# The three MLP blocks in two halves, with fewer and longer bursts of score maxima

## The chip, the cores and the metric

The kernel runs on one core of a Trainium2 chip. The time is the device time of that core in microseconds (us). The kernel before takes 1648.96 us, the median of three runs (1647.39 to 1649.14). The core's engines run their own instruction streams: TensorE (PE, with its weight loads shown as PEld), VectorE (DVE), ScalarE (ACT), GpSimd (POOL), and SyncE (SP), which here issues the DMAs. An engine takes its instructions in the order of the program, and waits where one needs the result of another engine.

## The reference: one transformer layer

For 2048 rows of 512 numbers:

```python
h   = x + attention(layernorm(x), wqkv) @ wo      # 32 heads of 16, softmax over all 2048 keys
out = h + silu(layernorm(h) @ w1) @ w2            # w1 is 512 x 1792, w2 is 1792 x 512
```

All arrays are float32, and the result has to keep float32 accuracy. The kernel therefore splits most operands of a product into a high and a low float16 part and adds three products (high with high, low with high, high with low).

## The kernel before, in words

**Attention.** The queries are taken in four blocks of 512 rows (`NB = 4`). Work is ordered in items: an item is four heads of one block, so there are 32 items (`ITEMS`), eight to a block. An item has 16 groups, one for each 128 keys (`KC = 16`). A group computes four score tiles of 128 keys by 512 queries (`scores`, line 414: one matmul and one exponential on ACT each), and, two groups later (`LAG = 2`), the products of the exponentials with the values (`values`, line 749), which add up in the PSUM bank `pv`.

**Maxima.** The exponential needs the maximum of each row of scores beforehand. `maximum` (line 259) computes a tile of 128 queries by 512 keys of the scores on PE, with 48 rows of contraction, into a PSUM bank, and DVE reduces it to one column (line 271). There are 64 such maxima to an item, 2048 in all. They run ahead of the attention that needs them, for items whose queries and keys are already loaded. When those of an item are complete, POOL turns them into two float16 rows (`finish_max`), and some steps later `place_max` transposes these on PE (`ps_n`), copies them on DVE (`mt`) and sends them by DMA into the query tile. Inside attention, a planner (`maxima`, line 1154) decides for each group how many maxima go beside its four scores, at most three, from the number still missing before each item's start; it takes off what the MLPs will do (`BESIDE`). `one_max` alternates between two heads whose rows lie in different halves of the array, rows 0 to 63 and 64 to 127. A maximum writes into one of the three `sm` banks in turn, or into a bank given by the caller.

**MLP.** When a block's attention is complete, its output projection and layer norm run beside the next block's first item, and the block's MLP runs in one piece at the start of the next item (`marks`: groups 144, 272 and 400; `finish_block`, line 1037, calls `mlp`, line 970). So three MLPs, called b = 0, 1, 2 here, stand between stretches of attention; the fourth, `finish_last`, ends the kernel and is written separately.

The MLP walks over the 1792 hidden features in 14 chunks of 128 (`FC = 14`). For chunk f, the *first product* is 12 matmuls of 128x128 by 128x512 (four slices of the 512 inputs, three float16 products each). `gate` then applies SiLU on ACT to a tile `g`, scales it to the high half of `gh` on ACT, and subtracts for the low half. The *second product* of the chunk (`second`, line 950) is again 12 matmuls, three for each 128 rows, into four banks `ps_acc`, in which all 14 chunks add up. Before the change, the loop runs first product of f, gate of f, second product of f - 1. The first product goes into `pv` (free at that time) and the four other banks of the kind `st` hold three accumulators and the chunk-0 product, then the fourth accumulator.

Between these matmuls stand bursts of maxima at fixed places (`BESIDE_C`): three after the 5th matmul of a first product, three after its 12th, and four after the 8th of a second product. `QUIET` leaves them out of the last three chunks of b = 2. At the end of each MLP eight scores of the coming groups are inserted.

**Order and time steps.** PE, ACT, DVE, POOL and SP instructions are kept in the order written. `tick()` counts steps, one for each chunk of the loop or group of attention, and `soon(n, ...)` puts off a small job by n steps: the placing of maxima, and the reciprocal of the softmax sums on POOL (`invert`, line 835) with its small DMAs.

**Weights.** The split w1 and w2 lie in DRAM and are loaded by `load_weights` into eight tiles of 256 KB (`raw_tile`), in the order of use. The exponentials and the gates' `gh` share a ring of tiles (`pt_tile`), twelve before the change (`PTS`).

Of the kernel before, what the change touches and what calls it, by code (L numbers as in the profile page):

```python
# [10 lines left out]
F32 = mybir.dt.float32  # L11
# [3 lines left out]
AF = mybir.ActivationFunctionType  # L15
ALU = mybir.AluOpType
# [4 lines left out]
P = 128  # L21
# [5 lines left out]
DC = D // P  # L27
FC = F // P
# [17 lines left out]


LAG = 2
PTS = 12

EARLY = 8

# [14 lines left out]
AHEAD = 4  # L67


BESIDE = (135, 135, 103)  # L70
OUTPUT = 9

BESIDE_V = [(0, 0), (0, 4, 4, 4)], [(4, 4), (4, 4, 4, 4)], [(6, 6), (6, 6, 6, 5)]
# [4 lines left out]

BESIDE_A1 = 10, 9, 8, 7

BESIDE_C = {5: 3, 12: 3}, {8: 4}

MORE = 2, 2, 0

QUIET = FC, FC, FC - 3


@with_exitstack
def attention_mlp_kernel(ctx: ExitStack, tc: tile.TileContext, x, wqkv, wo, w1, w2, out):
# [5 lines left out]
    def mm(*a, **k):  # L95
        tc.keep_in_program_order(nc.tensor.matmul(*a, **k))  # L96
# [5 lines left out]
    def pool(op, *a, **k):  # L102
        tc.keep_in_program_order(getattr(nc.gpsimd, op)(*a, **k))  # L103


    def pin(ins):
        tc.keep_in_program_order(ins)

    def act(fn, *a, **k):
        pin(getattr(nc.scalar, fn)(*a, **k))  # L110

    def dve(fn, *a, **k):
        pin(getattr(nc.vector, fn)(*a, **k))  # L113

    def dma(*a):
        pin(nc.sync.dma_start(*a))

    def low(dst, src, high, engine="dve"):

        if high.dtype == F32R:  # L120
            high = high.bitcast(F32)
        (pool if engine == "pool" else dve)("tensor_tensor", dst, src, high, ALU.subtract)
# [6 lines left out]
    def product(ps, lh, ll, rh, rl, n, start=True, stop=True):  # L129

        k = 0
        for c in range(n):
            for a, b in ((lh, rh), (ll, rh), (lh, rl)):
                mm(ps, a(c), b(c), start=start and k == 0, stop=stop and k == 3 * n - 1)
                k += 1
                yield
# [3 lines left out]
    small = ctx.enter_context(tc.tile_pool(name="small", bufs=3))  # L140
# [7 lines left out]
    def bank(name, kind="st", dtype=F32):  # L148
        pool_of = banks[kind]
        if isinstance(pool_of, list):  # L150
            pool_of.append(pool_of.pop(0))
            return pool_of[-1].tile([P, 512], dtype, tag=pool_of[-1].name, name=name)
        return pool_of.tile([P, 512], dtype, tag=kind, name=name)

    ident = const.tile([P, P], F32, name="ident")
# [16 lines left out]
    h_f, g_s, out_f, wo_f, o_minus, o_twice = (factors[:, n:n + 1] for n in range(8, 14))  # L172
# [128 lines left out]
    def finish_rest():  # L301
        while unfinished:
            finish_max(unfinished.pop(), True)
# [31 lines left out]
    def tick():  # L335
        at["step"] += 1
        for step in [step for step in late if step < at["step"]]:

            finish_rest()
            for i in late.pop(step):  # L340
                place_max(i)
        for fn, a in agenda.pop(at["step"], ()):
            fn(*a)
# [49 lines left out]
    def burst(n, *more):  # L393
        for ps in more:
            one_max(ps=ps)
        for _ in range(n - len(more)):
            one_max()

    def weave(steps, inserts):

        for k, _ in enumerate(steps):
            if k + 1 in inserts:
                inserts[k + 1]()
# [6 lines left out]
    def pt_tile(name, dtype=F32):  # L410
        pool_of = pools[next(taken) % PTS >= EARLY]
        return pool_of.tile([P, 512], dtype, tag="pt", name=name)
# [13 lines left out]
    with ExitStack() as pa:  # L426
# [289 lines left out]
        for g in range(1, NG // 2):  # L716
            for m, (b, key) in enumerate([(b, 1) for b in range(NB)] + [(b, 0) for b in range(NB)]):
# [3 lines left out]
                n = 8 * g + m - 12  # L721
# [16 lines left out]
    pv = bank("pv", "pv")  # L738
    cpool = ctx.enter_context(tc.tile_pool(name="cpool", bufs=1, side="right"))
    bp = ctx.enter_context(tc.tile_pool(name="bp", bufs=PTS - EARLY))  # L740
    pools.append(bp)
    gp = ctx.enter_context(tc.tile_pool(name="gp", bufs=2))
# [4 lines left out]
    hth = cpool.tile([P, DC, 512], F16, name="hth")  # L747
    htl = cpool.tile([P, DC, 512], F16, name="htl")
# [120 lines left out]
    ws, hx, os = {}, {}, {}  # L869


    first_weights = {9: ("w1", 0), 12: ("w1", 1), 14: ("w2", 0), 15: ("w1", 2)}

    def raw_tile():
        return gp.tile([P, 512], F32, tag="w", name="w", bufs=8)

    def parts_of(w):
        return w.bitcast(F16).rearrange("p (s n) -> p s n", s=2)

    def load_weights(kind, f):  # L880
        if f < FC:
            w = parts_of(raw_tile())
            dma(w, wd[kind][f])
            ws[kind, f] = w[:, 0], w[:, 1]
# [55 lines left out]
    def turn_rows(t):  # L940
        turn(hx.pop(t), hth[:, :, t * P:(t + 1) * P], htl[:, :, t * P:(t + 1) * P])

    def gate(ps):
        g, parts = pt_tile("g"), parts_of(pt_tile("gh"))
        act("activation", g, ps, AF.Silu, scale=h_f)
        act("mul", parts[:, 0], g, g_s)
        dve("scalar_tensor_tensor", parts[:, 1], g, g_s, parts[:, 0], op0=ALU.mult, op1=ALU.subtract)
        return parts[:, 0], parts[:, 1]

    def second(b, acc, f, gh, gl, inserts={}):  # L950
        w2h, w2l = ws.pop(("w2", f))
        while f == 0 and len(acc) < 4:
            acc.append(bank("ps_acc"))
        steps = (product(acc[t], lambda c: gh[:, t * P:(t + 1) * P], lambda c: gl[:, t * P:(t + 1) * P],
                         lambda c: w2h, lambda c: w2l, 1, start=f == 0, stop=f == FC - 1) for t in range(4))
        if f < FC - 1:
            weave(chain.from_iterable(steps), inserts)
            return
        for t, step in enumerate(steps):
            weave(step, {k - 3 * t: fn for k, fn in inserts.items()})  # L960
            n = 4 * b + t
            h = rows_of(b, t)

            parts = 1 + (n == KC - 1)
            for m in range(parts):
                cols = slice(m * D // parts, (m + 1) * D // parts)
                dve("scalar_tensor_tensor", h[:, cols], acc[t][:, cols], out_f, h[:, cols], op0=ALU.mult, op1=ALU.add)
                dma(out[n * P:(n + 1) * P, cols], h[:, cols])

    def mlp(b):  # L970

        first = bank("ps_w1")
        acc = [bank("ps_acc") for _ in range(3)]
        waiting = None
        ahead = [(g, m ^ (g % 2)) for g in marks[b:b + 1] + [marks[b] + 1] for m in range(4)]

        def some_scores(n):
            for _ in range(n):
                scores(*ahead.pop(0), "sm")

        for f in range(FC):
            tick()
            beside_1, beside_2 = BESIDE_C if f < QUIET[b] else ({}, {})
            beside_1 = {k: (lambda n=n: burst(n)) for k, n in beside_1.items()}
            if f == 0 and beside_1:

                beside_1[3] = lambda: burst(4, pv)
                del beside_1[5]
            beside_2 = {k: (lambda n=n: burst(n, *[pv] * (n == 4))) for k, n in beside_2.items()}
            if f == FC - 1:  # L990
                beside_2 = {8: lambda: some_scores(3)}
            if f:
                load_weights("w1", f + 2)
                load_weights("w2", f + 1)
            w1h, w1l = (w.rearrange("p (c n) -> p c n", n=P) for w in ws.pop(("w1", f)))

            ps = pv if f else first
            weave(product(ps, lambda c: w1h[:, c, :], lambda c: w1l[:, c, :],
                          lambda c: hth[:, c, :], lambda c: htl[:, c, :], DC), beside_1)

            parts = gate(ps)
            if f == FC - 1:

                act("activation", small.tile([P, 1], F32, name="sw"), ident[:, :1], AF.Exp)
            if waiting:
                second(b, acc, *waiting, beside_2)
            waiting = f, *parts

        def last_scores():

            scores(*ahead.pop(0))
            scores(*ahead.pop(0), "sm")
            if f < QUIET[b]:
                burst(2)

        second(b, acc, *waiting, {2: lambda: some_scores(3), 10: last_scores})

    found = {}

# [17 lines left out]
    def finish_block(b, pending):  # L1037

        act("activation", small.tile([P, 1], F32, name="sw"), ident[:, :1], AF.Silu)
        load_weights("w2", 1)  # L1040
        for g in pending:
            values(g)
        mlp(b)
# [110 lines left out]
    def maxima(g):  # L1154
# [4 lines left out]
        ready = min(ITEMS, i + RING - (0 if c == KC - 1 else 1)) * 64  # L1159
        rate = max([(n - sum(x for x, m in zip(BESIDE, marks) if g <= m <= start) - at["done"])  # L1160
                    / max(1, start - AHEAD - g) for n, start in goals] or [0])
# [14 lines left out]
    for g in range(groups):  # L1176
        tick()
        i, c = divmod(g, KC)
# [5 lines left out]
        if g < DC:  # L1184
            w = raw_tile()
            dma(w, wo[g * P:(g + 1) * P, :])
            soon(8, split_wo, g, w)
        f, c4 = divmod(g - SPLIT, 4)
        if c4 == 0 and 0 <= f < 2 * FC:
            kind, f = ("w1", "w2")[f % 2], f // 2  # L1190
            soon(4, split_weights, kind, f, load_raw(kind, f))
        if i in FIRSTS:
            b, n = i // 8 - 1, c - OUTPUT
# [23 lines left out]
        n = maxima(g)  # L1217
# [9 lines left out]
        for m in range(4):  # L1227
            k = m ^ (g % 2)
# [50 lines left out]
```

## Time and profile before

| | |
|---|---|
| median of three runs | 1648.96 us (1647.39 to 1649.14) |
| the profiled execution | 1649.26 us |
| its span, first to last instruction | 1647.5 us |
| PE busy | 1624.0 us, 99% |
| DVE busy | 1439.0 us, 87% |
| ACT busy | 1206.6 us, 73% |
| POOL busy | 363.5 us, 22% |
| MLPs b = 0, 1, 2, from first product to last | 497.6 to 601.6, 867.8 to 971.7, 1236.7 to 1335.7 us |

Times in the profile count from the span's start. A line of the timeline gives the start, the length, the engine, the line of the kernel, the operation, what it writes and reads, and how many like it follow one another; a bracket at its end is idle time of the engine before it, and what ended that. Matmuls are pipelined: a 512-column matmul shows a length of 0.38 us, but the next may begin earlier, so starts tell more than lengths. `PEclk` is the clock granted to PE, where 1.00 is full speed.

### The profile page before, as it was taken

To read this page: it belongs to the slowest core of one execution; us is meant where nothing else is said; L and a number is where in the kernel's file an instruction comes from. 1 tells how busy PE (TensorE), PEld (TensorE's weight loads), DVE (VectorE), ACT (ScalarE), POOL (GpSimd) and SP (SyncE) were. 2 spreads that over 40 slices of the span, in tenths; PEclk is the share of its full clock that TensorE was granted. 3 is DMA by queue.
4 is the path that set the end of the run, shared out by engine and by line. 5 is a ranking of instruction groups with operands and counts; after the bars stand their busy time and mean duration, and the time that the engine had idled before them with its cause. 6 is when DMAs were issued, how large, how long until landed. Compare 5 with 4: busy or idle time off the path is not lost.

```text
span 1647.5 us, 28474 instructions
## 1 busy us (share of the span) xinstructions
PE 1624.0 (99%) x10553; PEld 516.1 (31%) x10553; DVE 1439.0 (87%) x2385; ACT 1206.6 (73%) x2391; POOL 363.5 (22%) x594
## 2 busy tenths in 40 slices
PE   9899999999999999999999999999999999999999
PEld 7566522222223322222223322222233322222254
DVE  7799999999999989999999989999988969999431
ACT  5445599999972169999972169999972179999732
POOL 4323354544421001121121001121121001111100
PEclk9999999999999999999999999999999999999999
DMA  5657344333432211111232211112132211100222
GB/s 192 170 142 220 100 96 121 99 107 107 117 76 85 71 51 32 34 36 49 54 76 85 70 51 32 33 36 53 51 77 90 65 50 32 36 12 21 72 81 73
DMA packets 100951, 125.91 MB, mean 76 GB/s; under 512 B 24144, under 2 KB 61072, under 8 KB 100812
## 3 DMA queue, kind: packets, MB, share of 16 engines
q1 hardware_dynamic: 100812, 124.10, 27.1%
q8 instruction: 82, 1.34, 0.3%
q14 instruction: 57, 0.47, 0.1%
HBM read 93.45 MB, written 24.63 MB: 72 GB/s over the span
## 4 chain that ended last, share of the span: by engine, by line
PE 79%; DVE 14%; ACT 4%; DMA 2%; issue 1%; POOL 0%; SPq 0%; DVEq 0%; ACTq 0%
PE pv L96 32%; PE ps_s L96 21%; DVE mx L271 11%; PE ps_m L96 10%; PE ps_qk L96 5%; PE ps_acc L96 4%; PE ps_w L96 3%; ACT pt L110 3%; PE ps_wo L96 2%; PE ps_v L96 2%; DVE gh L113 1%; DMA ks<-in_B_w_dram 1%; PE ps_tr L99 1%; DVE ot L113 0%; DVE pvs L113 0%
## 5 line engine op out<-in xcount | busy, mean ns | idle before, releaser
L271 DVE TENSOR_REDUCE mx<-ps_m 128x1 f32<-128x512 f32 x2011 | 1260.5, 683 | 68.1 <-PE ps_m L96 36.4
L110 ACT ACTIVATE pt<-ps_s 128x512 f32<-128x512 f32 x2048 | 1010.4, 608 | 30.0 <-PE ps_m L96 17.8
L96 PE MATMUL pv<-pt,va 128*17 128x512 f32 x4096 | 537.6, 598 | 0.9
L96 PE MATMUL ps_s<-qs,ks 64*128 64x512 f16 x2048 | 532.6, 379 | 2.0 <-ACT pt L110 0.5
L96 PE MATMUL ps_m<-ks,qs 48*128 48x512 f16 x2011 | 513.6, 381 | 9.0 <-DVE mx L271 6.1
L96 PEld LDWEIGHTS <-ks 64*128 64x128 f16 x2048 | 150.3, 95 | 550.0 <-issue 437.1
L110 ACT ACTIVATE g<-pv,factors 128x512 f32<-128x512 f32 x39 | 26.8, 688 | 217.5 <-PE pv L96 217.5
L96 PE MATMUL ps_acc<-w,gh 128*128 128x512 f16 x672 | 161.2, 380 | 0.0
L103 POOL TENSOR_TENSOR ri<-rc,minus 128x16 f32<-128x16 f32 x31 | 90.9, 2932 | 282.0 <-DMA rc<-dn 282.0
L96 PEld LDWEIGHTS <-qs 48*128 48x128 f16 x2048 | 119.6, 94 | 76.1 <-issue 70.1
L96 PEld LDWEIGHTS pv<-pt,va 128*17 128x17 f32 x4096 | 69.0, 95 | 215.3 <-issue 202.7
L103 POOL TENSOR_TENSOR mx<-mx 128x32 f32<-128x32 f32 x34 | 8.6, 254 | 403.5 <-DVE mx L271 402.0
L113 DVE SCALAR_TENSOR_TENSOR gh<-g,factors,gh 128x512 f16<-128x512 f32 x56 | 41.7, 745 | 63.7 <-ACT gh L110 63.7
L96 PEld LDWEIGHTS <-w 128*128 128x128 f16 x708 | 65.2, 98 | 93.6 <-issue 29.1
L96 PE MATMUL pv<-hth,w 128*128 128x512 f16 x312 | 92.9, 379 | 0.0
L96 PEld LDWEIGHTS <-gh 128*128 128x128 f16 x672 | 59.2, 98 | 95.1 <-issue 32.4
L110 ACT ACTIVATE ks<-ps_qk,qk_s 128x512 f32<-128x512 f32 x30 | 20.7, 689 | 53.3 <-PE ps_qk L96 45.7
L96 PE MATMUL pv<-htl,w 128*128 128x512 f16 x156 | 59.5, 381 | 0.0
L103 POOL TENSOR_SCALAR nm<-nm 128x16 f32<-128x16 f32 (+1 forms) x50 | 13.1, 261 | 198.7 <-DVE nm L282 195.7
L96 PE MATMUL ps_qk<-xth,wqk_h 128*128 128x512 f32 x128 | 53.6, 419 | 0.6 <-ACT va L110 0.6
L96 PE MATMUL ps_qk<-xth,wqk_l 128*128 128x512 f32 x128 | 50.7, 396 | 0.0
L103 POOL TENSOR_TENSOR sl<-ks,sh 128x512 f16<-128x512 f32 x30 | 34.8, 1161 | 70.4 <-ACT sh L110 56.9
(134 smaller groups left out, 1002.8 us busy)
## 6 DMA issues: line engine op xcount, KB each, us to landing
ks<-kd SPq DMA_DIRECT2D x120, 192.0 KB
w<-w1d SPq DMA_DIRECT2D x56, 256.0 KB
w<-w2d SPq DMA_DIRECT2D x56, 256.0 KB
ks<-in_B_w_dram SPq DMA_DIRECT2D x28, 256.0 KB
w<-in_B_w_dram SPq DMA_DIRECT2D x28, 256.0 KB
qs<-qd SPq DMA_DIRECT2D x128, 48.0 KB
kd<-sh SPq DMA_DIRECT2D x16, 256.0 KB
qd<-sh SPq DMA_DIRECT2D x16, 256.0 KB
```

Of the source, the lines that this page charges most:

```text
L96: tc.keep_in_program_order(nc.tensor.matmul(*a, **k))
L99: tc.keep_in_program_order(nc.tensor.transpose(*a))
L103: tc.keep_in_program_order(getattr(nc.gpsimd, op)(*a, **k))
L110: pin(getattr(nc.scalar, fn)(*a, **k))
L113: pin(getattr(nc.vector, fn)(*a, **k))
L271: pin(nc.vector.tensor_reduce(mx[piece][:, j, a % n, qt, kb:kb + 1], ps, axis=AX.X, op=ALU.max))
```

## The change

The MLPs' loop is cut in two. First all 14 first products and gates run; the 14 tiles `gh` stay in the ring, which grows from 12 to 16. Then all 14 second products run. `g` gets two tiles of its own. In these three MLPs the low half of `gh` is made on POOL in two operations (scale `g` in place, subtract the high half) instead of one on DVE; the last MLP keeps DVE. Each first product writes a bank of the kind `st` in turn instead of `pv`.

The bursts change with it. In the first half there is one burst of six after the 6th matmul of a first product, not at chunks 6 and 13, and in b = 2 not at chunks 0, 3, 6, 9 and 12; it writes `pv`, two `st` banks and the three `sm` banks. In the second half, bursts of four (`pv` and three `sm`) are spread evenly over the first 144 matmuls: 16, 15 and 13 of them in b = 0, 1, 2. The planner's `BESIDE` becomes 138, 134, 106; the counts that really run in the MLPs were 135, 135 and 107 and become 138, 134 and 106.

Weights are loaded in the order all w1, then all w2, one a step and five ahead of use. There are now 28 steps (`tick`) in an MLP instead of 14. The activation-table switch to the exponential comes after the last gate, at the middle of the MLP instead of near its end.

```diff
-PTS = 12
+PTS = 16
-BESIDE = (135, 135, 103)
+BESIDE = (138, 134, 106)
-BESIDE_C = {5: 3, 12: 3}, {8: 4}
+BURSTS_1 = ({f: 6 for f in range(FC) if f not in (6, 13)},) * 2 + ({f: 6 for f in range(FC) if f % 3},)
+BURSTS_2 = 16, 15, 13
+SPAN_2 = 12 * (FC - 2)
-QUIET = FC, FC, FC - 3
...
-    first_weights = {9: ("w1", 0), 12: ("w1", 1), 14: ("w2", 0), 15: ("w1", 2)}
+    first_weights = {9: ("w1", 0), 12: ("w1", 1), 14: ("w1", 2), 15: ("w1", 3)}
+    order = [(kind, f) for kind in ("w1", "w2") for f in range(FC)]
...
-    def gate(ps):
-        g, parts = pt_tile("g"), parts_of(pt_tile("gh"))
+    def gate(ps, engine="dve"):
+        g, parts = gp.tile([P, 512], F32, name="g"), parts_of(pt_tile("gh"))
         act("activation", g, ps, AF.Silu, scale=h_f)
         act("mul", parts[:, 0], g, g_s)
-        dve("scalar_tensor_tensor", parts[:, 1], g, g_s, parts[:, 0], op0=ALU.mult, op1=ALU.subtract)
+        if engine == "pool":
+            pool("tensor_scalar", g, g, g_s, 1.0, op0=ALU.mult, op1=ALU.mult)
+            low(parts[:, 1], g, parts[:, 0], "pool")
+        else:
+            dve("scalar_tensor_tensor", parts[:, 1], g, g_s, parts[:, 0], op0=ALU.mult, op1=ALU.subtract)
...
     def mlp(b):
...
-            ps = pv if f else first
+            ps = bank("ps_w1")
+            n = BURSTS_1[b].get(f, 0)
             weave(product(ps, lambda c: w1h[:, c, :], lambda c: w1l[:, c, :],
-                          lambda c: hth[:, c, :], lambda c: htl[:, c, :], DC), beside_1)
-
-            parts = gate(ps)
-            if f == FC - 1:
-
-                act("activation", small.tile([P, 1], F32, name="sw"), ident[:, :1], AF.Exp)
-            if waiting:
-                second(b, acc, *waiting, beside_2)
-            waiting = f, *parts
...
+                          lambda c: hth[:, c, :], lambda c: htl[:, c, :], DC),
+                  {6: lambda: burst(n, pv, bank("ps_m"), bank("ps_m"))} if n else {})
+            gates.append(gate(ps, "pool"))
+
+        act("activation", small.tile([P, 1], F32, name="sw"), ident[:, :1], AF.Exp)
+        acc = []
+        inserts = {SPAN_2 * (n + 1) // BURSTS_2[b]: lambda: burst(4, pv) for n in range(BURSTS_2[b])}
+        inserts[12 * (FC - 2) + 8] = inserts[12 * (FC - 1) + 2] = lambda: some_scores(3)
+        inserts[12 * (FC - 1) + 10] = last_scores
+        for f in range(FC):
+            tick()
+            next_weights()
+            second(b, acc, f, *gates[f], {k: inserts[12 * f + k] for k in range(1, 13) if 12 * f + k in inserts})
...
-        load_weights("w2", 1)
+        load_weights("w1", 4)
```

More of the change, by code (lines that the diff above doesn't have):

```diff
@@ L970, in mlp, with next_weights @@
     def mlp(b):
-        first = bank("ps_w1")
-        acc = [bank("ps_acc") for _ in range(3)]
-        waiting = None
         ahead = [(g, m ^ (g % 2)) for g in marks[b:b + 1] + [marks[b] + 1] for m in range(4)]
+        weights = iter(order[5:])
+        def next_weights():
+            for kind, f in weights:
+                load_weights(kind, f)
+                return
         def some_scores(n):
@@ L979, in some_scores @@
                 scores(*ahead.pop(0), "sm")
[L981 to L989, printed above, removed]
-            if f == FC - 1:
[L991 to L995, printed above, removed]
-            ps = pv if f else first
-            weave(product(ps, lambda c: w1h[:, c, :], lambda c: w1l[:, c, :],
-                          lambda c: hth[:, c, :], lambda c: htl[:, c, :], DC), beside_1)
-            parts = gate(ps)
-            if f == FC - 1:
-                act("activation", small.tile([P, 1], F32, name="sw"), ident[:, :1], AF.Exp)
-            if waiting:
-                second(b, acc, *waiting, beside_2)
-            waiting = f, *parts
         def last_scores():
@@ L1012, in last_scores @@
             scores(*ahead.pop(0), "sm")
-            if f < QUIET[b]:
+            if b < 2:
                 burst(2)
-        second(b, acc, *waiting, {2: lambda: some_scores(3), 10: last_scores})
+        gates = []
+        for f in range(FC):
+            tick()
+            next_weights()
+            w1h, w1l = (w.rearrange("p (c n) -> p c n", n=P) for w in ws.pop(("w1", f)))
+            ps = bank("ps_w1")
+            n = BURSTS_1[b].get(f, 0)
+            weave(product(ps, lambda c: w1h[:, c, :], lambda c: w1l[:, c, :],
+                          lambda c: hth[:, c, :], lambda c: htl[:, c, :], DC),
[6 more added lines that the diff above has]
+        inserts[12 * (FC - 1) + 10] = last_scores
+        for f in range(FC):
+            tick()
+            next_weights()
+            second(b, acc, f, *gates[f], {k: inserts[12 * f + k] for k in range(1, 13) if 12 * f + k in inserts})
     found = {}
```

## The prediction

> **What bounds the kernel now.** I read the page's engine shares first, then a table of stretches for the places that the change touches and for an attention between them, then one period of an MLP in the timeline.
>
> ```profile
> PE 1624.0 (99%) x10553; PEld 516.1 (31%) x10553; DVE 1439.0 (87%) x2385; ACT 1206.6 (73%) x2391; POOL 363.5 (22%) x594
> ```
>
> PE looks full everywhere, so only a stage's own rows tell its limit. The stretches (columns: time, then busy time of each engine with its instructions, granted clock, DMA share, GB/s):
>
> ```profile
> core 0: us, PE busy (x) PEld busy (x) DVE busy (x) ACT busy (x) POOL busy (x), PEclk, DMA share, GB/s
> 497.60:601.60 104.00, 102.76 (x485) 34.05 (x480) 94.03 (x153) 25.42 (x39) 8.40 (x22) 1.00 0.22 65
> ...
> 975.00:1205.00 230.00, 229.55 (x1757) 51.50 (x1753) 220.23 (x359) 229.29 (x467) 38.90 (x62) 1.00 0.18 44
> ```
>
> In attention (975 to 1205) ACT works 229.29 of 230 us: 467 exponentials and copies of 0.491 us set the pace, and PE keeps up. Nothing in the change shortens ACT's work there, so attention gains nothing. In the MLP ACT works only 25 of 104 us, PE nearly all, DVE 94. The clock is 1.00 in both. What PE spends in the MLP is read from one period (chunk 5 or so of b = 0):
>
> ```profile
> 527.17 0.38 PE L96 MATMUL pv<-htl,w 128*128 128x512 f16 x1
> ...
> 527.48 0.60 PE L96 MATMUL ps_m<-ks,qs 48*128 48x512 f16 x3
> ...
> 527.91 1.89 DVE L271 TENSOR_REDUCE mx<-ps_m 128x1 f32<-128x512 f32 x3 [0.50 <-PE ps_m L96]
> ...
> 528.02 1.90 PE L96 MATMUL ps_acc<-w,gh 128*128 128x512 f16 x8
> ...
> 529.85 0.39 PE L96 MATMUL pv<-ks,qs 48*128 48x512 f16 x1
> 529.86 0.60 PE L96 MATMUL ps_m<-ks,qs 48*128 48x512 f16 x3
> ...
> 530.39 1.04 PE L96 MATMUL ps_acc<-w,gh 128*128 128x512 f16 x4
> 530.97 3.78 DVE L271 TENSOR_REDUCE mx<-ps_m 128x1 f32<-128x512 f32 x6
> ...
> 532.44 0.83 PE L96 MATMUL ps_m<-ks,qs 48*128 48x512 f16 x3
> 533.20 1.19 PEld L96 LDWEIGHTS <-w 128*128 128x128 f16 x7 [0.66 <-issue]
> ...
> 534.82 0.60 PE L96 MATMUL ps_m<-ks,qs 48*128 48x512 f16 x3
> ```
> ```profile
> 1315.34 2.59 PE pv L96 x12
> 1317.93 2.59 PE ps_acc L96 x12
> ```
>
> The last two lines (chain of waits, the part of b = 2 without bursts) give a full matmul: 2.59 / 12 = 0.216 us. The maxima start in pairs, within 0.01 us of each other (529.85 and 529.86), since the two heads use different halves of the array. So n maxima take n/2 slots, rounded up, of 0.216 us: four lie between 529.85 and 530.39, which is 0.54 = two slots and 0.11. Three take just as long (527.48 to 528.02), an odd one leaving half a slot empty. The entry costs as much as the exit: the matmul at 527.17 should be followed after 0.216, the burst starts after 0.31. So **a burst costs 0.21 us beside its slots**. The Trainium skill (TensorEngine Tiling (Array Packing), section Key Properties) says that a change of the tiling mode drains the engine, without a price; by that rule, too, cost goes with the number of bursts, and the trace agrees with 0.21 us for the two changes of a burst.
>
> A period from 527.48 to 534.82 is 7.34 us: 24 x 0.216 = 5.18, six slots 1.30, three bursts 0.63, together 7.11. The missing 0.23 is at 532.44: the burst of three lasts until 533.20, 0.76 instead of 0.54, because its third maximum must wait for DVE to finish the third of the earlier burst of four (third of the six reduces from 530.97, start 532.22, end about 532.89). DVE is late there because the gate's operation stands in its queue.
>
> **The change, part by part.** Prices come from the profiled execution of 1649.26 us, 0.3 above the median. Rows for the three MLPs' ends, for other prices, and for a finishing of maxima on POOL (its first and last operation):
>
> ```profile
> 497.63 0.61 PE L96 MATMUL ps_w<-hth,w 128*128 128x512 f16 x2
> ...
> 601.13 0.61 PE L96 MATMUL ps_acc<-w,gh 128*128 128x512 f16 x2
> ```
> ```profile
> 867.77 0.60 PE L96 MATMUL ps_w<-hth,w 128*128 128x512 f16 x2
> ...
> 971.27 0.60 PE L96 MATMUL ps_acc<-w,gh 128*128 128x512 f16 x2
> ```
> ```profile
> 1236.74 0.61 PE L96 MATMUL ps_w<-hth,w 128*128 128x512 f16 x2
> ...
> 1331.89 1.28 PE L96 MATMUL ps_s<-qs,ks 64*128 64x512 f16 x3
> ...
> 1335.26 0.61 PE L96 MATMUL ps_acc<-w,gh 128*128 128x512 f16 x2
> ```
> ```profile
> L113 DVE SCALAR_TENSOR_TENSOR gh<-g,factors,gh 128x512 f16<-128x512 f32 x56 | 41.7, 745 | 63.7 <-ACT gh L110 63.7
> L110 ACT ACTIVATE gh<-g,factors 128x512 f16<-128x512 f32 x56 | 40.4, 721 | 1.8
> L110 ACT ACTIVATE g<-pv,factors 128x512 f32<-128x512 f32 x39 | 26.8, 688 | 217.5 <-PE pv L96 217.5
> L103 POOL TENSOR_SCALAR w<-w,factors 128x512 f32<-128x512 f32 x32 | 22.3, 695 | 26.1 <-DMA w<-in_B_w_dram 17.8 <-PE pv L96 6.2 <-DMA den<-dr 2.1
> L103 POOL TENSOR_TENSOR w<-w 128x512 f16<-128x512 f32 x28 | 32.5, 1161 | 2.4
> L103 POOL TENSOR_SCALAR ks<-ks,mv,rs 128x512 f32<-128x512 f32 x4 | 8.8, 2195 | 0.0
> L103 POOL TENSOR_TENSOR ri<-rc,minus 128x16 f32<-128x16 f32 x31 | 90.9, 2932 | 282.0 <-DMA rc<-dn 282.0
> ```
> ```profile
> 545.80 0.24 POOL L103 TENSOR_TENSOR mx<-mx 128x32 f32<-128x32 f32 x1 [36.72 <-DVE mx L271]
> ...
> 548.40 0.22 POOL L103 TENSOR_TENSOR ns<-nm,ns 128x16 f16<-128x16 f32 x1
> ```
>
> With 0.43 us for the last two matmuls the MLPs last 103.9, 103.9 and 98.95 us.
>
> *Full matmuls.* 336 in each MLP before and after: 72.6 us, no change.
>
> *Bursts and slots.* Before, b = 0 and 1 have 41 bursts with 81 slots each (chunk 0: bursts of 4 and 3; chunks 1 to 12: 3, 3, 4; chunk 13: 3, 3; one of 2 at the end), b = 2 has 32 with 64: 114 bursts, 226 slots. After: 12 of six, 16 of four and one of two make 29 bursts with 69 slots; 12, 15 and one make 28 with 67; 9 and 13 make 22 with 53. One burst of six, at a change of item, takes heads in the order 1, 0, 0, 0, 1, 0 and needs a fourth slot: 79 bursts, 190 slots in all. Saved: 35 x 0.21 = 7.4 and 36 x 0.216 = 7.8, together **15.1 us**. One maximum more in all (378 for 377) moves out of attention, where ACT sets the pace: nothing.
>
> *Waits for DVE.* Before: the lengths less 72.6, less bursts and slots (26.1, 26.1, 20.5), less the eight scores at the end (three inserts, four slots: 1.5) leave 3.7, 3.7 and 4.3. Placing maxima inside takes about 0.3 of the first two and 0.6 of the last, so waits are about 3.4, 3.4 and 3.7, **10.5 us**. In b = 2 this holds a wait of the scores at 1331.89 (1.28 for 0.60), behind gates and the table switch on ACT that come much earlier after the change.
> After, first half: PE needs 12 x 0.216 + 3 x 0.216 + 0.21 = 3.45 us from burst to burst, but DVE six reduces, 6 x 0.625 = 3.75 (the 3.78 above, less its tail). So DVE sets the pace wherever bursts follow in successive chunks. The reduces begin 0.43 us after a burst's start (527.48 to 527.91); the sixth ends at 0.43 + 5 x 0.625 + 0.67 = 4.22, and the next burst's sixth maximum, due at 3.45 + 0.43 = 3.88, waits 0.34, each further one 0.30. Six bursts in a row cost 0.34 + 4 x 0.30 = 1.55, twice in b = 0 and 1: 3.1 each; b = 2 has bursts in pairs, 4 x 0.34 = 1.4. The chunk without a burst lets DVE catch up (2.59 more). In the second half PE needs 9 x 0.216 + 0.43 + 0.21 = 2.58 and DVE 4 x 0.625 = 2.50: one wait of 0.2 at the start, then none. In b = 1 a placing stands half a product (1.3) after a burst, whose fourth reduce, that of its bank, ends 0.9 later. Together 3.3 + 4.2 + 1.4 = **8.9 us**: not removed, only moved. Bounds: none at all (the bursts before show 0.23 at most places without this lock), or double.
>
> *The gates on POOL.* 0.695 + 1.161 = 1.86 us a chunk by the nearest rows of the same shape and scalars, behind ACT's 0.69 + 0.72. The period is 3.75, so POOL is busy half the time; nobody needs the low half before the second half begins. `g` has two tiles, so the SiLU of f waits if POOL isn't through with f - 2. Queued on POOL among them are a reciprocal (2.93 and three small ones, 3.8 in all) and a finishing of maxima (some 2.8): each delays the next gate by less than one period, and the two-tile slack holds. From below it can gain nothing further: DVE's 0.745 a chunk, gone from its queue, is already in the pace above. From above: were the scaling to take the 2195 ns of another POOL form, a gate takes 3.36; 12 gates, and 7 for the others, make 47 us, as long as the half: 1 to 2 us an MLP. I take zero.
>
> *Banks.* A first product takes a fresh `st` bank; two of the four others go to maxima. Product f + 1's burst reuses product f's bank 1.3 us after its end; SiLU is through after 0.9. The fourth accumulator reuses the last product's bank after nine matmuls, 1.9 us. Zero, with 0.4 and 1.0 us of cover.
>
> *DMAs.* The same 28 loads an MLP, one a step; five steps ahead are at least 13 us (5 x 2.59), and the DMA share is 0.22. On SP's queue the store of the reciprocals, which now waits behind five gates on POOL, holds up the load of chunk 10 by some 4 us of those 13. Zero, and `mt`'s DMAs come two each as before.
>
> *Steps.* Placings come three steps later, now 10 us instead of 22; finishing takes POOL some 5 with a gate ahead. As many `ps_n` as before, six: zero.
>
> *Ring of 16, table switch earlier, the last MLP.* ACT sets attention's pace, so more tiles bring nothing; the last MLP's order is unchanged.
>
> Sum: 15.1 + 10.5 - 8.9 = 16.7 us. 1649.26 - 16.7 = 1632.6; against the median, 1632.3. I say **1632.5**.
>
> **The rivals.**
> *DVE's lock costs more* (or POOL's queue adds to it): if each full burst in the first half waits some 0.6, and placings more, the waits double to 18: 1641.5. For it: DVE at 94 of 104 us. Against it: the 3.78 row shows DVE running six reduces without a gap while PE waits.
> *No lock*: the waits vanish: 1624.
> *No change*: the MLP's gain is taken back by attention, as when ACT waits for keys or placed maxima that came with the MLP's length: 1649. Against it: ACT's 229.29 of 230 follow an MLP directly.
> *POOL becomes the bound, and the kernel slower.* Fourteen gates go to the engine that needs 1.86 for what DVE does in 0.745. It decides where 12 gates and 7 us exceed the half (about 47) by the 5.5 saved in each MLP, at 3.8 us a gate. At double the rows' price, 3.7, the gain is just lost; at 4.5, twelve of them and 7 are 61, 14 us over the half: 1632.5 + 42 = 1675. The Trainium skill (GPSIMD Engine Reference, section Elementwise — side-by-side cycle accounting) says that DVE stays the rule for elementwise work, GpSimd being about half as fast; the rows agree, but price it at half a period. The other way to this end is that POOL's work blocks DVE's reduces. A stretch with POOL busy 63 of 125 us shows that it doesn't (least, median and longest reduce in ns; columns of the second row as above):
>
> ```profile
> L271 DVE TENSOR_REDUCE mx<-ps_m x187: 677/681/693, 205.4 to 329.8; 128x1 f32<-128x512 f32 x187
> ```
> ```profile
> 205.00:330.00 125.00, 124.94 (x959) 28.16 (x959) 119.66 (x194) 125.00 (x256) 63.01 (x94) 1.00 0.39 105
> ```
>
> **How the numbers follow.** The likeliest 0.70 (1629 to 1637 on its own); lock doubled 0.11; no lock 0.05; no change 0.05; POOL as bound 0.09. Leaving out the slower end and the no-change case, the range runs from 1625 (no lock) to 1645 (lock doubled, with 1 to 2 us an MLP from POOL). A difference under 0.2% (3.3 us) can't be told from none here: faster 0.86, same 0.05, slower 0.09.
>
> **What would show it.** Right: in the timeline, bursts of six 3.75 apart in the first half, with the reduces unbroken for six chunks; 2.6 apart in the second; MLPs of about 99, 99 and 92.5 us; attention with ACT full as before. Wrong: SiLU waiting for POOL, PE waiting for `w` tiles, reduces longer than 0.68, or gaps in ACT just after an MLP.

## The result and the profile after

The changed kernel takes 1630.38 us, the median of four runs (1629.9 to 1630.93), beside 1648.68 us for the kernel before (now the median of four runs, hence not the 1648.96 above). The ratio is 0.9887, with a 95% interval of 0.9875 to 0.9899: 18.3 us less, where 16.7 were forecast. The forecast of 1632.5 us is 2.1 us too high; the measured time lies inside the range of 1625 to 1645 us.

The first lines of the page of the kernel after, with the engines' shares:

```profile
span 1628.1 us, 28586 instructions
## 1 busy us (share of the span) xinstructions
PE 1609.1 (99%) x10553; PEld 518.3 (32%) x10553; DVE 1408.7 (87%) x2340; ACT 1207.2 (74%) x2391; POOL 443.7 (27%) x696
```

PE does the same 10553 instructions and still shows 99%. DVE lost 30 us and POOL gained 80, nearly all of it by the 42 gates. None of this tells where 19.4 us of span went. That is read from the starts and ends of the three MLPs in the timeline (first matmul of a first product, and first of the last two second products, as in the prediction):

| | before | after | difference |
|---|---|---|---|
| start of b = 0 | 497.63 | 496.49 | -1.14 |
| length of b = 0 | 103.50 | 98.12 | -5.38 |
| attention between b = 0 and 1 | 266.64 | 266.69 | +0.05 |
| length of b = 1 | 103.50 | 97.87 | -5.63 |
| attention between b = 1 and 2 | 265.47 | 265.11 | -0.36 |
| length of b = 2 | 98.52 | 91.83 | -6.69 |
| from there to the end | 312.24 | 311.99 | -0.25 |

The MLPs give 17.7 us, the attention between and after 0.6. I do not count the 1.1 us ahead of the first MLP as the change's: the shift is there in the first 75 us already, where the two programs are alike, and over all profiles of this case that MLP starts between 495.09 and 499.84, in no order of the kernels (in the chains of waits, the same product `ps_v` starts at 72.45 before and at 71.25 after).

The rows of the kernel after on which the table rests, first and last of each MLP:

```profile
496.49 0.61 PE L96 MATMUL ps_w<-hth,w 128*128 128x512 f16 x2
...
594.61 0.61 PE L96 MATMUL ps_acc<-w,gh 128*128 128x512 f16 x2
...
861.30 0.60 PE L96 MATMUL ps_w<-hth,w 128*128 128x512 f16 x2
...
959.17 0.61 PE L96 MATMUL ps_acc<-w,gh 128*128 128x512 f16 x2
...
1224.28 0.60 PE L96 MATMUL ps_w<-hth,w 128*128 128x512 f16 x2
...
1316.11 0.60 PE L96 MATMUL ps_acc<-w,gh 128*128 128x512 f16 x2
```

A period of the first half, in the timeline of the kernel after (some rows between left out):

```profile
505.05 0.39 PE L96 MATMUL pv<-ks,qs 48*128 48x512 f16 x1
505.05 0.95 PE L96 MATMUL ps_m<-ks,qs 48*128 48x512 f16 x5
505.40 0.69 POOL L103 TENSOR_SCALAR g<-g,factors 128x512 f32<-128x512 f32 x1 [1.77 <-ACT gh L110]
505.50 0.68 DVE L271 TENSOR_REDUCE mx<-pv 128x1 f32<-128x512 f32 x1
505.94 0.60 PE L96 MATMUL ps_w<-hth,w 128*128 128x512 f16 x2
506.10 3.07 DVE L271 TENSOR_REDUCE mx<-ps_m 128x1 f32<-128x512 f32 x5
506.18 1.16 POOL L103 TENSOR_TENSOR gh<-g,gh 128x512 f16<-128x512 f32 x1
...
508.63 0.39 PE L96 MATMUL pv<-ks,qs 48*128 48x512 f16 x1
...
509.09 0.68 DVE L271 TENSOR_REDUCE mx<-pv 128x1 f32<-128x512 f32 x1
```

The burst starts at 505.05 and the product goes on at 505.94: 0.89 us for three slots (0.65), the change back to full matmuls (0.10) and 0.14 of waiting. The second burst of each run of six waits longer: 1.01 us from 501.34 to 502.35, so 0.26. From burst to burst it is 3.58 to 3.59 us, and the reduces follow without a gap: one into the next from 505.50, six in 3.59. So DVE does set the pace here, as forecast, but with 0.598 us a reduce rather than 0.625. The second half of b = 0:

```profile
547.00 0.60 PE L96 MATMUL ps_m<-ks,qs 48*128 48x512 f16 x3
547.53 2.12 PE L96 MATMUL ps_acc<-w,gh 128*128 128x512 f16 x9
549.58 0.39 PE L96 MATMUL pv<-ks,qs 48*128 48x512 f16 x1
549.59 0.74 PE L96 MATMUL ps_m<-ks,qs 48*128 48x512 f16 x3
550.26 2.12 PE L96 MATMUL ps_acc<-w,gh 128*128 128x512 f16 x9
```

Bursts of four take 0.53 and 0.68 us in turn (547.00 to 547.53; 549.58 to 550.26): every second one waits 0.14 for its fourth bank. The stretch of the first half of b = 0 (columns as in the prediction):

```profile
496.50:544.90 48.40, 48.40 (x246) 17.97 (x241) 43.44 (x73) 18.91 (x27) 28.71 (x39) 1.00 0.28 83
```

DVE has 43 of 48 us of work there, and POOL 29.

### The profile page after: what moved, and what is told of

The parts are those of the page before. It is cut to its first block, busy times and chain, and to the rows that moved or that the text cites. A ratio compares the mean times of both kernels' runs of the same rounds, so it can differ in the third digit from the quotient of the medians.

```text
span 1628.1 us, 28586 instructions
## 1 busy us (share of the span) xinstructions
PE 1609.1 (99%) x10553; PEld 518.3 (32%) x10553; DVE 1408.7 (87%) x2340; ACT 1207.2 (74%) x2391; POOL 443.7 (27%) x696
## 4 chain that ended last, share of the span: by engine, by line
PE 88%; DVE 6%; ACT 4%; DMA 1%; issue 1%; POOL 0%; SPq 0%; DVEq 0%; ACTq 0%
PE pv L96 30%; PE ps_s L96 22%; PE ps_m L96 9%; PE ps_acc L96 9%; PE ps_w L96 8%; PE ps_qk L96 5%; DVE mx L271 4%; ACT pt L110 3%; PE ps_wo L96 2%; PE ps_v L96 2%; DMA ks<-in_B_w_dram 1%; PE ps_tr L99 1%; DVE st L113 0%; PE ps_n L99 0%; DVE ot L113 0%
## 5 line engine op out<-in xcount | busy, mean ns | idle before, releaser
L271 DVE TENSOR_REDUCE mx<-ps_m 128x1 f32<-128x512 f32 x1971 | 1232.9, 682 | 53.8 <-PE ps_m L96 23.3
L96 PE MATMUL ps_m<-ks,qs 48*128 48x512 f16 x1971 | 499.3, 380 | 5.5 <-DVE mx L271 5.2
L96 PE MATMUL ps_acc<-w,gh 128*128 128x512 f16 x672 | 157.2, 380 | 0.0
L110 ACT ACTIVATE g<-ps_w,factors 128x512 f32<-128x512 f32 x56 | 38.5, 687 | 127.6 <-PE ps_w L96 123.3
L96 PE MATMUL ps_w<-hth,w 128*128 128x512 f16 (+1 forms) x472 | 132.9, 369 | 0.0
L271 DVE TENSOR_REDUCE mx<-pv 128x1 f32<-128x512 f32 x77 | 52.9, 687 | 42.6 <-PE ps_m L96 41.2
L96 PE MATMUL ps_w<-htl,w 128*128 128x512 f16 (+1 forms) x236 | 83.9, 368 | 0.0
L113 DVE SCALAR_TENSOR_TENSOR gh<-g,factors,gh 128x512 f16<-128x512 f32 x14 | 10.5, 752 | 52.1 <-ACT gh L110 52.1
```

Of the source, the lines that this page charges most:

```text
L271: pin(nc.vector.tensor_reduce(mx[piece][:, j, a % n, qt, kb:kb + 1], ps, axis=AX.X, op=ALU.max))
```

## The experiments

Three things changed at once: the order of the products with its bursts, the engine of the gates' low half, and the ring. What came along with the order (the loads' order, the two tiles of `g`, the earlier table switch) was not run alone. A ratio compares a run with the kernel before, run beside it on the same chip. Lengths of MLPs are read as in the table above; in the two profiles of the changed kernel they repeat to 0.01 us, so they tell more than the medians, which carry the shifting start.

**The ring alone**, in the kernel before:

```diff
-PTS = 12
+PTS = 16
```

> The kernel before with the ring of 16 tiles in place of 12, nothing else. Theory (ACT sets the pace of attention): 1648.7, no change. Rival (the longer ring lets ACT run ahead and brings part of the gain): 1645 or less.

Measured: 1649.65 us, beside 1649.68 for the kernel before; ratio 1.0002 (0.9993 to 1.0012). The ring only makes room for the 14 tiles.

**The gates' low half on POOL alone**, in the kernel before:

```diff
-    def gate(ps):
+    def gate(ps, engine="dve"):
...
-            parts = gate(ps)
+            parts = gate(ps, "pool")
```

What `gate` does for `"pool"` is as in the change.

> The kernel before with only the gates' low half moved to POOL, loop and bursts as they were. Theory: only the waits for DVE shrink, from 0.23 to about 0.1 a period and at the first bursts: 33 x 0.13 + 1 to 2 = 5 to 6 us, 1643 (1641 to 1646). Rival (the move to POOL is the gain, the order of products is not): 1631.

Measured: 1647.37 us, ratio 0.9988 (0.9979 to 0.9998): some 2 us less instead of the 5 to 6 that I expected. The MLPs' lengths are 102.36, 102.36 and 98.67 us, so 1.14 less in two of them and 0.15 more in b = 2. Its timeline, at the place of the wait shown in the prediction:

```profile
528.79 0.60 PE L96 MATMUL ps_m<-ks,qs 48*128 48x512 f16 x3
529.33 1.04 PE L96 MATMUL ps_acc<-w,gh 128*128 128x512 f16 x4
...
531.38 0.75 PE L96 MATMUL ps_m<-ks,qs 48*128 48x512 f16 x3
532.06 0.39 PE L96 MATMUL pv<-htl,w 128*128 128x512 f16 x1
```

The burst at 531.38 still takes 0.68 in place of 0.54. With the gate gone from DVE's queue, the third maximum still waits for its bank: a burst of four and one of three, 2.6 us apart, share three `sm` banks. The wait went from 0.23 to 0.14. Most of it hangs on the spacing and the banks, not on the gate.

**The gates back on DVE**, in the changed kernel:

```diff
-            gates.append(gate(ps, "pool"))
+            gates.append(gate(ps))
```

> The changed kernel with the low half of gh made on DVE again in the three MLPs. Theory (PE pays 0.21 us a burst and 0.216 a slot, and DVE sets the pace where bursts of six follow each other): DVE then needs 6 x 0.60 + 0.745 = 4.34 us a chunk in the first half, where it needs 3.59 now, so each run of six bursts loses 4 us: 8 us in b = 0 and 1, 2 to 3 us in b = 2, together 18: 1648 to 1650, the whole gain gone. Rival (the gain is the fewer bursts alone, and DVE has slack): 1631, no change.

Measured: 1644.77 us, ratio 0.9976 (0.9967 to 0.9986): 4 us of the gain are left. The MLPs take 104.00, 104.34 and 93.77 us; nearly all of the increase is in the first halves, 54.26 for 48.45 in b = 0. Its timeline:

```profile
505.42 0.68 DVE L271 TENSOR_REDUCE mx<-pv 128x1 f32<-128x512 f32 x1
506.02 3.06 DVE L271 TENSOR_REDUCE mx<-ps_m 128x1 f32<-128x512 f32 x5
...
509.01 0.73 DVE L113 SCALAR_TENSOR_TENSOR gh<-g,factors,gh 128x512 f16<-128x512 f32 x1
509.13 0.37 PE L96 MATMUL ps_m<-ks,qs 48*128 48x512 f16 x1 [0.23 <-DVE mx L271]
509.67 0.67 DVE L271 TENSOR_REDUCE mx<-pv 128x1 f32<-128x512 f32 x1
```

Six reduces and a gate make a period of 4.25 us (505.42 to 509.67), DVE has no gap, and PE waits for the sixth bank. The mechanism holds, but the time lies below the 1648 to 1650 forecast: beside the changed kernel the MLPs lost 14 us where I said 18. A gate takes 0.66 of DVE's queue rather than 0.745, and a run of six bursts lost 2.9 us (half of 54.26 less 48.45) rather than 4. So the move to POOL is worth 2 us in the old order and 14 in the new one: it is what lets the new order's first half run.

**Smaller bursts in the second halves**: each of four cut into two and two, or into three and one.

```diff
-        inserts = {SPAN_2 * (n + 1) // BURSTS_2[b]: lambda: burst(4, pv) for n in range(BURSTS_2[b])}
...
+            k = SPAN_2 * (n + 1) // BURSTS_2[b]
+            inserts[k - 4] = lambda: burst(2, pv)      # or burst(3, pv)
+            inserts[k] = lambda: burst(2)              # or burst(1)
```

> The changed kernel, each burst of four in the second halves cut into two bursts of two, four matmuls apart: 44 bursts more, no slot more. Theory: 44 x 0.21 = 9.2 us more, less some waits of 0.14 that end: 1638 to 1640. Rival (the price of a burst is its maxima only): 1630.5, no change.

> The changed kernel, each burst of four in the second halves cut into three and one: 44 bursts more and 44 slots more. Theory: 44 x (0.21 + 0.216) = 18.7 us more, less up to 2 us of waits: 1647 to 1649. Rival (an odd maximum costs no more than an even one): as with twos, 1638 to 1640.

Measured: 1638.18 us (ratio 0.993, 0.9913 to 0.9946) and 1647.61 us (ratio 0.9991, 0.9981 to 1.0001). Both are as forecast. The price is cleanest in the second half of b = 2, where no burst waits: 46.53 us with 13 bursts of four, 48.94 with twos, 51.65 with threes and ones. The 46.53 holds one wait that the other two do not have: three scores near the end take 0.90 us (1311.12 to 1312.02) where they take 0.53 with twos (1321.43 to 1321.96), as with threes and ones. Without these 0.37 us a burst more costs 2.78 / 13 = 0.214 us, and a burst and a slot more 5.49 / 13 = 0.422. Timelines there, first of the changed kernel, then of the twos, then of three and one:

```profile
1272.05 0.60 PE L96 MATMUL ps_m<-ks,qs 48*128 48x512 f16 x3
1272.59 2.55 PE L96 MATMUL ps_acc<-w,gh 128*128 128x512 f16 x11
1275.07 0.39 PE L96 MATMUL pv<-ks,qs 48*128 48x512 f16 x1
...
1311.12 0.39 PE L96 MATMUL ps_s<-qs,ks 64*128 64x512 f16 x2
1311.71 0.37 PE L96 MATMUL ps_s<-qs,ks 64*128 64x512 f16 x1 [0.20 <-DVE mx L271]
1312.02 1.47 PE L96 MATMUL ps_acc<-w,gh 128*128 128x512 f16 x6
```
```profile
1281.95 0.39 PE L96 MATMUL ps_m<-ks,qs 48*128 48x512 f16 x1
1282.27 1.04 PE L96 MATMUL ps_acc<-w,gh 128*128 128x512 f16 x4
1283.24 0.39 PE L96 MATMUL ps_m<-ks,qs 48*128 48x512 f16 x2
1283.57 1.68 PE L96 MATMUL ps_acc<-w,gh 128*128 128x512 f16 x7
1285.18 0.39 PE L96 MATMUL pv<-ks,qs 48*128 48x512 f16 x1
...
1321.43 0.60 PE L96 MATMUL ps_s<-qs,ks 64*128 64x512 f16 x3
1321.96 1.47 PE L96 MATMUL ps_acc<-w,gh 128*128 128x512 f16 x6
```
```profile
1287.04 0.39 PE L96 MATMUL ps_m<-ks,qs 48*128 48x512 f16 x1
1287.36 1.69 PE L96 MATMUL ps_acc<-w,gh 128*128 128x512 f16 x7
```

Eleven full matmuls and four maxima take 3.02 us as one burst and 3.23 as two. A lone maximum holds PE from 1287.04 to 1287.36, as long as the pair at 1283.24 does until 1283.57.

**Threes in the first halves**:

```diff
+                  {4: lambda: burst(3, pv, bank("ps_m"), bank("ps_m")), 10: lambda: burst(3)} if n else {})
-                  {6: lambda: burst(n, pv, bank("ps_m"), bank("ps_m"))} if n else {})
```

> The changed kernel, each burst of six in the first halves cut into two of three (after the 4th and the 10th matmul): 33 bursts and 33 slots more. Theory: 33 x 0.43 = 14.1 us more on PE, but PE's 3.88 us a chunk is then above DVE's 3.59, so about 4 us of waits end: 1639 to 1641. Rival (DVE sets the first half's pace anyway, so PE's extra work is hidden): 1631 to 1632.

Measured: 1640.5 us, ratio 0.9947 (0.993 to 0.9963). The MLPs take 101.60, 100.74 and 94.60, and the time is as forecast. This kernel tells most about the sum. It has nearly the bursts and slots of the kernel before (112 and 222, for 114 and 226), and yet its three MLPs are 8.6 us shorter together, far more than two bursts and four slots are worth (1.3 us). The rest, about 7 us by subtraction, is waits that are gone: with the new order, its banks and the gates on POOL every burst of the first halves takes 0.53 to 0.54 us, so none waits. From here to the changed kernel, sixes for threes give another 9.1 us in the MLPs: 14.1 less of switching and slots, and some 5 of waits that come back because DVE then sets the pace.

**More work on POOL**, two multiplications by one in each gate:

```diff
             pool("tensor_scalar", g, g, g_s, 1.0, op0=ALU.mult, op1=ALU.mult)
+            for _ in range(2):
+                pool("tensor_scalar", g, g, ones[:, :1], 1.0, op0=ALU.mult, op1=ALU.mult)
```

> The changed kernel with two more multiplications by one of g on POOL in each gate of the three MLPs: 0.69 us each, 3.25 a gate for 1.86. Theory (POOL is off the path as long as a gate takes less than the 3.6 us of a chunk): 1630.5 to 1632. Rival (POOL's lateness reaches ACT by the two tiles g, and so PE): 12 x 1.39 = 17 us an MLP less what the chunk hides, 1640 or more.

Measured: 1646.8 us, ratio 0.9984 (0.9974 to 0.9993), so 16 us more than the changed kernel. My theory failed and the rival held. The MLPs take 102.26, 101.21 and 98.18, 13.8 us more together. The list of waits of this kernel (us in total, times, longest), its timeline late in the first half of b = 0, at that half's end and at the end of b = 1's, and a stretch (columns as in the prediction) just behind the wait at 548.03:

```profile
ACT g L110 <- POOL gh L103: 62.7, 23, 6.0
```
```profile
531.34 0.69 ACT L110 ACTIVATE g<-ps_w,factors 128x512 f32<-128x512 f32 x1 [2.04 <-POOL gh L103]
...
548.03 0.29 PE L99 MATMUL ps_n<-ident_h,ns 128*32 128x128 f16 x1 [2.35 <-POOL ns L103]
548.25 3.60 PE L96 MATMUL ps_acc<-w,gh 128*128 128x512 f16 x9
...
551.50 0.69 ACT L110 ACTIVATE g<-ps_w,factors 128x512 f32<-128x512 f32 x1 [4.82 <-POOL gh L103]
...
921.20 2.32 PE L96 MATMUL ps_acc<-w,gh 128*128 128x512 f16 x10 [2.13 <-ACT g L110]
```
```profile
548.20:551.20 3.00, 3.00 (x8) 1.04 (x8) 0.21 (x1) 0.00 (x0) 2.73 (x4) 0.50 0.07 12
```

For five chunks the pace stays at 3.59. Then the reciprocal stands 4 us in POOL's queue, SiLU waits for a free tile `g` (as at 531.34), and POOL, at 3.47 us a gate, cannot make up the delay. At the end of b = 0's first half PE waits 2.35 us for the finished maxima, which stand behind gates. The nine matmuls behind that wait take 3.60 us for 2.12, and this is no further wait: the granted clock was 0.50 there. At the end of b = 1's first half the fourth accumulator waits 2.13 us for the last SiLU, which frees its bank. PE's five long waits in the three MLPs (2.35; 1.46 and 2.13; 3.06 and 1.37) make 10.4 us, and the half clock, which also followed the wait of 3.06, took some 1.5 twice: 13.4 of the 13.8. A queue need not be full on average to cost: it was 3.47 of 3.59.

**Bursts of six spread evenly** over the first half, with 15 instead of 16 fours in b = 0:

```diff
-BURSTS_1 = ({f: 6 for f in range(FC) if f not in (6, 13)},) * 2 + ({f: 6 for f in range(FC) if f % 3},)
-BURSTS_2 = 16, 15, 13
-BESIDE = (138, 134, 106)
+BURSTS_1 = ((6, 19, 32, 45, 58, 71, 84, 100, 113, 126, 139, 152),) * 2 + ((6, 23, 40, 57, 76, 93, 112, 129, 148),)
+BURSTS_2 = 15, 15, 13
+BESIDE = (134, 134, 106)
...
-                  {6: lambda: burst(n, pv, bank("ps_m"), bank("ps_m"))} if n else {})
+                  {k - 12 * f: lambda: burst(6, pv, bank("ps_m"), bank("ps_m")) for k in BURSTS_1[b]})
```

> The changed kernel with the first half's bursts of six spread evenly over its matmuls (13 or 14 apart, and 17 in b = 2) in place of 12 apart with gaps, and 15 instead of 16 bursts of four in b = 0. Theory: PE needs 13 x 0.216 + 0.86 = 3.67 us from burst to burst, more than DVE's 3.59, so the waits of the first half go, 1.6 us in b = 0 and 1 and 1.0 in b = 2, and with one burst less and fewer waits in the second half of b = 0 another 1.2: 1625 (1624 to 1627). Rival (DVE's total work decides, not where the bursts stand): 1630.

Measured: 1630.65 us, ratio 0.989 (0.9874 to 0.9907): no gain over the changed kernel, where 1624 to 1627 was forecast. The MLPs became shorter as forecast, 95.55, 95.56 and 91.38 us, together 5.3 less. But attention between them took 267.74 and 266.58 us, 1.05 and 1.47 more, and the rest to the end 1.5 more. The list of waits and the timeline show what took it:

```profile
PEld L96 <- DMA qs<-mt: 6.1, 4, 1.7
```
```profile
808.71 0.22 PE L99 MATMUL ps_n<-ident_h,ns 128*32 128x128 f16 x1 [0.16 <-DVE mx L271]
...
812.55 0.39 PE L96 MATMUL ps_s<-qs,ks 64*128 64x512 f16 x1 [0.81 <-DMA qs<-mt]
```

Scores at three starts of items wait for the placed maxima, 0.81 to 0.83 us each; in the one shown the transpose came only 3.8 us earlier. Two readings were possible: four maxima fewer ahead, or the new places of the bursts. The next run put the four back and kept the places, with the changed kernel once more beside it:

```diff
-BURSTS_2 = 15, 15, 13
-BESIDE = (134, 134, 106)
+BURSTS_2 = 16, 15, 13
+BESIDE = (138, 134, 106)
```

> The changed kernel with the first half's bursts of six spread as in the run spread, but with all 16 bursts of four in b = 0, so that as many maxima as in the changed kernel lie in the MLPs (138, 134, 106). Theory: in spread the MLPs became 5.3 us shorter, and attention gave 4 us back in three waits for placed maxima, because four maxima fewer were done ahead; with 138 these waits go and the MLPs stay 4.1 us shorter than the changed kernel's (1.4, 2.3 and 0.4): 1626 to 1627, or 0.9865 of the kernel before. Rival (the waits for placed maxima come from where the bursts stand in the MLP, not from their number): they stay, 1629 to 1631.

> The changed kernel once more, beside spread138 on the same chip: 1630 to 1631 by either theory, and MLPs of the same lengths as in its first profile within 0.1 us.

Measured: 1628.33 us for the spread (ratio 0.9877, 0.986 to 0.9893) and 1631.97 for the changed kernel (0.9901, 0.9884 to 0.9917), each a little above its forecast. Attention is back at 266.69 and 265.11 us, to the hundredth that of the changed kernel, so it was the number of maxima done ahead. The MLPs take 96.71, 97.01 and 91.02, together 3.1 us less than the 98.12, 97.87 and 91.82 of the changed kernel's second profile; 4.1 were expected, but in b = 1 a placing waits 1.17 us for its bank. The two intervals overlap, so the medians alone do not prove this version faster; the lengths of the MLPs with unchanged attention do show its 3 us. Its median is the lowest of the case.

## Why the prediction was right

*The limit of each stage.* Right. Attention neither gained nor lost more than 0.4 us a stretch, and the gain sits in the MLPs: 5.4, 5.6 and 6.7 us, where my lengths of 99, 99 and 92.5 for 103.9, 103.9 and 98.95 meant 4.9, 4.9 and 6.5.

*Bursts and slots, 15.1 us.* Right. The twos price a burst at 0.214 us, and three and one price burst and slot at 0.422, against 0.21 and 0.43; with these the term is 15.0. The threes in the first half cost 9.9 us by the ratios, between the 8.5 and 10.5 forecast.

*The waits.* The mechanism was right, but the 8.9 us after were too many, so the gain forecast was a little too small. I took 10.5 us before and 8.9 after. With the same subtraction as in the prediction (336 full matmuls, bursts, slots, scores, two placings) the lengths after leave 2.9, 3.2 and 1.5, together 7.6. The mis-sized term is DVE's pace, 0.598 us a reduce where I took 0.625: the first locked burst of a run waits 0.26, not 0.34, and each further one 0.14, not 0.30. I had read 0.625 from a row of six reduces in 3.78 us as if it had no gap; its fourth reduce had in truth waited for a maximum that PE began only at 532.44, and started 0.695 after the third, the others 0.60 apart. Against that, in the second half of b = 0 every second burst waits 0.14, and in b = 1 five of 15, where I had one wait. The placing in b = 1 waited 0.62 us, where I said 0.9:

```profile
907.68 0.22 PE L99 MATMUL ps_n<-ident_h,ns 128*32 128x128 f16 x1 [0.62 <-DVE mx L271]
```

*DVE's queue as the cause of the waits before.* Only half right. I wrote that DVE is late because the gate's operation stands in its queue; taking it away in the old order left 0.14 of 0.23. The bursts' spacing and the three banks keep the rest.

*The gates on POOL, zero.* Right, at 0.694 + 1.156 us, and in the whole kernel the profile puts only two waits of SiLU down to POOL, 2.1 us each, no longer than its usual wait for a product (2.15). But the rival was nearer than I made it. I said that 3.36 us a gate would cost 1 to 2 us an MLP, and that the gain is lost at 3.7 to 3.8. The run with 3.25 us of work a gate (3.47 from gate to gate) lost 16 us by the medians, so nearly all: the sum of busy times missed that one late gate delays the next two, that the finished maxima and the last SiLU stand in the same line, and that the clock was halved behind two of PE's waits.

*Banks, DMAs, steps, ring.* No wait of PE for a gate's bank or for a `w` tile shows in the kernel after, and the ring alone changes nothing (1.0002). One count was wrong: the MLPs hold six placings (`ps_n`) after but four before, not six, which costs 0.6 us at the 0.3 each that I took. So the sum closes: 15.1 + 10.5 - 7.6 - 0.6 = 17.4 us, beside the 17.7 by which the MLPs became shorter. The medians differ by 18.3; the rest is 0.6 us outside the MLPs and the shifting start.

## What to carry to other kernels

A small matmul between large ones is paid by the burst and the slot, not by its size: here 0.21 us for each burst (its two changes together) and 0.216 us for each started pair, so fill bursts to an even number and make them as long as the free banks allow. Longer bursts need as many banks and an even spacing, or the evacuating engine sets the pace; whatever else that engine does in the stretch, even 0.66 us a period, then lands on the path. And work that runs ahead under one stage is credit for the next: four maxima fewer there cost 4.0 us in attention, more than the 3.1 that the spreading wins.

## What the runs showed of the hardware beside this

Reduces of 128x512 from PSUM that follow each other without a wait start every 0.598 us although each shows 0.68, so the length of a row overstates the pace by 14%. A matmul that waits for a bank starts within 0.05 us of the end of the reduce that frees it: 509.13 in the run with the gates on DVE, where the reduces before end at 506.02 + 3.06 = 509.08. POOL's scaling of 128x512 by one column and a constant takes 0.694 us, within 0.001 of the row for another tile that the prediction priced it by. In the run with more work on POOL the granted clock was 0.50 and 0.52 in the 3 us behind PE's waits of 2.35 and 3.06 us, with matmuls 0.43 us apart in place of 0.216; behind a wait of 2.13 us it was 1.00.
